# The first layer's gate, s*relu(h)^2 + b, formed whole in the elementwise steps

## The chip, the cores and the metric

One core of a Trainium2 chip runs the whole kernel. The metric is the device time of one execution in microseconds (us); a difference of 2% gets a verdict. The core has a matrix engine (TensorE, PE in the profile; its weight loads are PEld), VectorE (DVE), ScalarE (ACT) and GpSimd (POOL), and an engine that only issues transfers here (SyncE, SP). Each takes its instructions from a queue of its own, in order.

## The reference, cut to what matters

Attention with a memory term gives x; the first layer and the second layer follow. All arrays are float32.

```python
def _moe_ref(x, w_in, w_out, s, b):      # x (2304, 512), w_in (512, 2048), w_out (2048, 512)
    h = x @ w_in
    r = np.maximum(h, 0.0)
    g = s * (r * r) + b                  # s and b: one number each
    return (g @ w_out).astype(np.float32)

def _moe2_ref(x, w_in, w_out):           # the same sizes
    h = x @ w_in
    ...
    g = h * np.tanh(sp)                  # sp = log(1 + exp(h))
    return (g @ w_out).astype(np.float32)
```

Attention has 4 x 8 pairs of batch and head, 576 positions and 64 dimensions of a head.

## The kernel before, in words

**Precision.** TensorE is fed in the 32-bit format `fp32r`. To keep float32 accuracy each operand is split in a high part, rounded to that format, and a low part, the rest; a product takes three matmuls (high x high, high x low, low x high). The splitting is elementwise work: a cast makes the high part, a subtraction the low part.

**Stages.** Attention is done in units, one for a batch and head; batch 0 is done first, in smaller pieces, the other 24 units follow. Meanwhile the weights of the first layer, which arrive as 64-bit words, are converted (`convert`, L602 to L631: load by SyncE into one of the `raw` buffers, two steps on ScalarE, L609 and L614, two on VectorE, L616 and L617, an addition on GpSimd, L619). As soon as the first 256 columns of x are there, the first layer starts between the units of attention. When attention is done, the first layer has TensorE to itself, while the weights of the second layer are converted in the same way and stored to DRAM (L631); there are two `raw` and two `w` buffers, and the load of a conversion stands in SyncE's queue behind the store of an earlier one. Then they are read back, split (L640, L642), and the second layer runs.

**The first layer.** It goes over 9 blocks of 256 tokens (j) and in each over 16 chunks of 128 of the 2048 hidden columns (fc), 144 chunks in all. For a chunk TensorE makes h in a bank of PSUM (`h`, two banks), three parts of four matmuls (L677). `first` then forms the gate in four steps: ScalarE writes relu(h) to `rt` (L705), VectorE multiplies max(h, 0) by it (L706, which also frees the bank), ScalarE casts to `gh` (L708), VectorE subtracts to `gl` (L709). Three chunks later `y_part` multiplies gh and gl by the output weights `woh` and `wol` (12 matmuls, L722) into y. So the gate that TensorE sees is r*r, without s and b. The factor s is put on when y leaves PSUM (`y_out`, L735 on ScalarE and L737 on VectorE, two each for a block). The term b adds b times the column sum of the output weights to each column of y. `column_sums` makes these sums: VectorE adds all 16 slices of woh and wol into `total` (31 additions of 512 columns, L652 and L654), TensorE sums over partitions by a matmul with `ones` (L670), VectorE picks the diagonal and multiplies by b into `bcs` (L666, L668). When the second layer loads y (`load_y`), the cast to `yh` has bcs as its bias (L767) and the subtraction to `yl` adds it too (L770).

**What sets the order.** No engine chooses at run time. Every step is added to a plan with its engine, an estimated duration, a priority, what it waits for and the buffers it needs. `Plan.order` (L168) plays these estimates through before the program is built: a free engine takes the ready step of lowest priority number, and buffers are rings that are waited for. The order in which steps are taken is the order of the instructions in each queue. `column_sums` has priority 700, the loads of y 450, the conversions of the second layer 655.2, the matmuls of the first layer 1000 and more, its elementwise steps -1. The estimates are those of the code (0.264 us for L705, 0.307 for L708), not those of the chip.

Of the kernel before, what the change touches and what calls it, by code (L numbers as in the profile page):

```python
# [9 lines left out]
F32 = mybir.dt.float32  # L10
# [4 lines left out]
AF = mybir.ActivationFunctionType  # L15
ALU = mybir.AluOpType
# [3 lines left out]
P = 128  # L20
# [32 lines left out]
def dve_us(n, fast=False):  # L53
    return 0.068 + (0.00052 if fast else 0.00104) * n
# [200 lines left out]
def attention_then_two_ffn(ctx: ExitStack, tc: tile.TileContext, qk, qz, vm, beta,  # L255
# [3 lines left out]
    nc = tc.nc  # L259
# [34 lines left out]
    ones = const.tile([P, P], F32, name="ones")  # L294
    igate = const.tile([P, 2, H], F32, name="igate")
    sb = const.tile([P, 2], F32, name="sb")
    bcs = const.tile([P, NCC], F32, name="bcs")
# [8 lines left out]
    sums_in = Buf()  # L306
# [10 lines left out]
    nc.scalar.activation(ones, mask[:, :P], AF.Copy, bias=1.0)  # L317
# [327 lines left out]
    def column_sums(prio):  # L645

        total, ps = Buf(R["total"], [P, 512]), Buf(R["o2"], [P, 512])

        def more(r, j, nm):
            x = W[1, nm, r].t[:, j, :].bitcast(F32)  # L650
            if r == j == 0 and nm == "wol":
                nc.vector.tensor_tensor(total.t, W[1, "woh", 0].t[:, 0, :].bitcast(F32), x, op=ALU.add)  # L652
            elif r + j:
                nc.vector.tensor_tensor(total.t, total.t, x, op=ALU.add)  # L654

        for r in range(NR):
            for j in range(FPR):
                def pair(r=r, j=j):
                    more(r, j, "woh")
                    more(r, j, "wol")  # L660

                add(DVE, dve_us(512) * (2 if r + j else 1), prio, pair, [W[1, "woh", r], W[1, "wol", r]] + [total] * (r + j > 0), [total])

        def pick():
            for ec in range(NCC):
                nc.vector.tensor_tensor_reduce(total.t[:, ec * P:(ec + 1) * P], ps.t[:, ec * P:(ec + 1) * P], ident, 1.0, 0.0,  # L666
                                               ALU.mult, ALU.add, bcs[:, ec:ec + 1])
            nc.vector.tensor_scalar(bcs, bcs, sb[:, 1:2], None, op0=ALU.mult)  # L668

        add(PE, 0.87, prio, lambda: nc.tensor.matmul(ps.t, ones, total.t, start=True, stop=True), [total], [ps])  # L670
        add(DVE, 1.0, prio, pick, [ps, total], [sums_in, total])

# [23 lines left out]
    def first(j, fc, prio, ew):  # L696
# [8 lines left out]
        add(ACT, 0.264, ew, lambda: nc.scalar.activation(rt.t, ph.t[:, :N1], AF.Relu), [ph], [rt])  # L705
        add(DVE, 0.335, ew, lambda: nc.vector.scalar_tensor_tensor(rt.t, ph.t[:, :N1], 0.0, rt.t, op0=ALU.max, op1=ALU.mult),  # L706
            [ph, rt], [rt])
        add(ACT, 0.307, ew, lambda: nc.scalar.copy(gh.t, rt.t), [rt], [gh])  # L708
# [214 lines left out]
```

## Time and profile before

| what | us |
|---|---|
| median of three runs (lowest, highest) | 1129.08 (1126.43, 1130.62) |
| the profiled execution: its time | 1132.63 |
| the profiled execution: span from first to last instruction | 1130.5 |
| TensorE busy | 1066.4 (94%) |
| VectorE busy | 686.3 (61%) |
| ScalarE busy | 545.1 (48%) |
| GpSimd busy | 279.7 (25%) |

A share of busy time is a mean over stages that differ: up to about 509 us attention with the first layer between, to about 715 us the first layer alone, then the second. TensorE's matmuls overlap, so that its busy time says little of how near it is to its peak; its waits say more. Three kinds of rows are read below: busy time in a stretch, what ended an engine's idle time ("PE h L677 <- DVE rt L706" reads: the matmul of line 677 waited for the rt that VectorE writes in line 706), and the chain of work that ended last, followed back from the end.

### The profile page before, as it was taken

The numbers are of one execution on the slowest core, as the hardware profiler recorded it, in microseconds if no ns is written. First come the engines' busy times: TensorE is split into PE (matmuls) and PEld (weight loads), VectorE is DVE, ScalarE is ACT, GpSimd is POOL, SyncE is SP. The second block draws the span as 40 slices with busy tenths as digits, with TensorE's granted clock in tenths as the row PEclk, the third lists the DMA queues.
The fourth block names the chain that finished last, engine by engine and source line by source line (L and its number), as shares of the span: only waits on it lengthen the run. The fifth ranks groups of instructions, "written<-read, shape, count | busy, mean of one in ns | idle before, by whom it ended". The sixth has DMA issues, their size and how long they took to land.

```text
span 1130.5 us, 19718 instructions
## 1 busy us (share of the span) xinstructions
PE 1066.4 (94%) x6868; PEld 969.1 (86%) x6868; DVE 686.3 (61%) x2071; ACT 545.1 (48%) x1343; POOL 279.7 (25%) x361
## 2 busy tenths in 40 slices
PE   5879999998999999999899999999999999999998
PEld 3446788997989998998889999999999999999997
DVE  6898999999889888899964334632223232232221
ACT  6576887778778787774553324521112121111111
POOL 5763554455354534442221000000000000000000
PEclk9578999999999999999999999999999999999999
DMA  8463653534334432356563102500101000000000
GB/s 250 131 192 105 187 175 109 152 111 145 102 90 137 137 111 81 112 165 182 177 216 112 39 1 94 179 27 1 56 1 57 1 29 29 1 28 1 28 1 28
DMA packets 54963, 106.80 MB, mean 94 GB/s; under 512 B 6992, under 2 KB 34640, under 8 KB 54864
## 3 DMA queue, kind: packets, MB, share of 16 engines
q1 hardware_dynamic: 54864, 105.54, 30.3%
q8 instruction: 54, 0.88, 0.3%
q14 instruction: 45, 0.37, 0.1%
HBM read 82.97 MB, written 22.54 MB: 93 GB/s over the span
## 4 chain that ended last, share of the span: by engine, by line
PE 59%; DVE 13%; POOL 6%; ACT 6%; issue 5%; DMA 4%; SPq 0%; POOLq 0%; ACTq 0%; DVEq 0%
PE h L677 27%; PE o L795 17%; PE y L722 6%; POOL Pt L486 4%; PE o L722 2%; PE a L541 2%; PE a L513 2%; DVE gl L709 1%; DVE PTl L521 1%; DMA raw<-in_w_in 1%; ACT Pt L469 1%; DVE total L654 1%; DMA raw<-in_w_out 1%; DVE w L617 1%; DVE rt L706 1%
## 5 line engine op out<-in xcount | busy, mean ns | idle before, releaser
L784 ACT ACTIVATE g<-h 128x384 f32<-128x384 f32 x96 | 47.1, 491 | 309.2 <-PE h L677 285.7
L785 DVE CAST gh<-g 128x384 fp32r<-128x384 f32 x96 | 34.6, 361 | 263.6 <-ACT g L784 262.7
L513 PE MATMUL a<-ident,Pt 128*128 128x128 f32 x432 | 76.0, 295 | 31.9 <-POOL Pt L486 26.5
L619 POOL TENSOR_TENSOR w<-w,raw 128x512 int32<-128x512 int32 x54 | 72.9, 1349 | 123.5 <-DVE w L617 68.6
L677 PE MATMUL h<-xh,wih 128*128 128x256 f32 x576 | 95.1, 289 | 8.6 <-DVE rt L706 8.6
L486 POOL TENSOR_SCALAR Pt<-Pt,rs 128x64 f32<-128x64 f32 (+2 forms) x88 | 82.6, 963 | 66.1 <-DVE rs L491 50.4
L677 PE MATMUL h<-xl,wih 128*128 128x256 f32 x576 | 95.2, 287 | 0.1
L677 PE MATMUL h<-xh,wil 128*128 128x256 f32 x576 | 94.8, 287 | 0.0
L513 PEld LDWEIGHTS a<-ident,Pt 128*128 128x128 f32 x432 | 49.8, 146 | 51.8 <-POOL Pt L486 42.2
L469 ACT ACTIVATE Pt<-Pt,mx 128x64 f32<-128x64 f32 (+4 forms) x148 | 81.6, 552 | 23.4 <-DVE mx L460 23.0
L706 DVE SCALAR_TENSOR_TENSOR rt<-h,rt 128x256 f32<-128x256 f32 x144 | 60.4, 419 | 49.6 <-ACT rt L705 48.7
L709 DVE TENSOR_TENSOR gl<-rt,gh 128x256 fp32r<-128x256 f32 x144 | 69.4, 483 | 34.5 <-ACT gh L708 13.5
L677 PEld LDWEIGHTS h<-xh,wih 128*128 128x128 f32 x576 | 79.6, 193 | 11.6 <-DVE rt L706 11.0
L708 ACT CAST gh<-rt 128x256 fp32r<-128x256 f32 x144 | 58.2, 405 | 61.5 <-DVE rt L706 57.0
L472 POOL TENSOR_SCALAR Pt<-ex,nm 128x64 f32<-128x64 f32 x148 | 67.6, 469 | 77.4 <-PE a L513 37.7
L705 ACT ACTIVATE rt<-h 128x256 f32<-128x256 f32 x144 | 54.9, 381 | 59.6 <-PE h L677 56.6
L677 PE MATMUL h<-yh,wih 128*128 128x384 f32 x384 | 82.7, 337 | 0.0
L677 PE MATMUL h<-yl,wih 128*128 128x384 f32 x384 | 82.7, 337 | 0.0
L677 PE MATMUL h<-yh,wil 128*128 128x384 f32 x384 | 82.7, 337 | 0.0
L677 PEld LDWEIGHTS h<-xl,wih 128*128 128x128 f32 x576 | 80.2, 192 | 1.0 <-DVE xl L693 0.4
L677 PEld LDWEIGHTS h<-xh,wil 128*128 128x128 f32 x576 | 79.7, 192 | 0.9 <-issue 0.8
L795 PE MATMUL o<-wol,gh 128*128 128x512 f32 x285 | 80.3, 390 | 0.0
(177 smaller groups left out, 2565.7 us busy)
## 6 DMA issues: line engine op xcount, KB each, us to landing
qk<-in_qk SPq DMA_DIRECT2D x24, 608.0 KB, 3.9
raw<-in_w_out SPq DMA_DIRECT2D x28, 512.0 KB, 3.9
raw<-in_w_in SPq DMA_DIRECT2D x26, 512.0 KB, 4.8
qn<-in_qz SPq DMA_DIRECT2D x29, 192.0 KB, 2.4
vx<-in_vm SPq DMA_DIRECT2D x29, 160.0 KB, 2.4
xr<-x_d SPq DMA_DIRECT2D x36, 128.0 KB, 2.8
y_d<-ys SPq DMA_DIRECT2D x36, 128.0 KB, 1.7
yr<-y_d SPq DMA_DIRECT2D x24, 192.0 KB, 2.7
```

Source lines behind the costliest of these rows:

```text
L469: nc.scalar.activation(Pt[t].t[:, D:w + D], Pt[t].t[:, D:w + D], AF.Exp, bias=mx.t[:, t + i:t + i + 1], scale=-1.0, accum_out=rs.t[:, t:t ...
L472: add(POOL, 0.3, lambda: nc.gpsimd.tensor_scalar(Pt[t].t[:, :D], ex.t[:, t, :], nm.t[:, t:t + 1], 1.0, op0=ALU.mult, op1=ALU.mult), [ex, n ...
L486: (nc.vector if e == DVE else nc.gpsimd).tensor_scalar(x, x, r, None, op0=ALU.mult)
L513: nc.tensor.transpose(ps.t[:, c - c0, :], Pt[t].t[:, c * P:(c + 1) * P], ident)
L619: add(POOL, 1.23, prio, lambda: nc.gpsimd.tensor_tensor(w.t, w.t, words()[:, :, 0], op=ALU.add), [raw, low_words, w], [w])
L677: nc.tensor.matmul(ph, W[layer, nm, r].t[:, cc, o:o + P], x[:, cc], start=(part == 0 and cc == 0), stop=(part == 2 and cc == NCC - 1))
L705: add(ACT, 0.264, ew, lambda: nc.scalar.activation(rt.t, ph.t[:, :N1], AF.Relu), [ph], [rt])
L706: add(DVE, 0.335, ew, lambda: nc.vector.scalar_tensor_tensor(rt.t, ph.t[:, :N1], 0.0, rt.t, op0=ALU.max, op1=ALU.mult), [ph, rt], [rt])
L708: add(ACT, 0.307, ew, lambda: nc.scalar.copy(gh.t, rt.t), [rt], [gh])
L709: add(DVE, dve_us(N1), ew, lambda: nc.vector.tensor_tensor(gl.t, rt.t, gh.t.bitcast(F32), op=ALU.subtract), [rt, gh], [gl])
L722: nc.tensor.matmul(acc[ec // 2].t[:, (ec % 2) * N1:(ec % 2 + 1) * N1], W[1, nm, r].t[:, jj, ec * P:(ec + 1) * P], x.t, start=False, stop=( ...
L795: nc.tensor.matmul(acc[i].t, x.t[:, i * P:(i + 1) * P], W[2, nm, r].t[:, jj, :], start=(fc == 0 and part == 0), stop=(fc == NFC - 1 and pa ...
```

## The change

The gate is made whole: ScalarE writes s*h to `rt` (Copy with a scale read from memory), VectorE multiplies max(h, 0) by it, ScalarE adds b while it casts to `gh` (Identity with a bias read from memory), and VectorE adds b and subtracts gh in one step with three operands. `column_sums`, its tiles and its matmul are gone, y is copied out of PSUM without s, and y is loaded without a bias. Priorities and estimated durations of the steps that stay are as before.

```diff
-    ones = const.tile([P, P], F32, name="ones")
...
-    bcs = const.tile([P, NCC], F32, name="bcs")
...
-    nc.scalar.activation(ones, mask[:, :P], AF.Copy, bias=1.0)
...
-    def column_sums(prio):
-
-        total, ps = Buf(R["total"], [P, 512]), Buf(R["o2"], [P, 512])
...
-                add(DVE, dve_us(512) * (2 if r + j else 1), prio, pair, [W[1, "woh", r], W[1, "wol", r]] + [total] * (r + j > 0), [total])
...
-        add(PE, 0.87, prio, lambda: nc.tensor.matmul(ps.t, ones, total.t, start=True, stop=True), [total], [ps])
-        add(DVE, 1.0, prio, pick, [ps, total], [sums_in, total])
...
-        add(ACT, 0.264, ew, lambda: nc.scalar.activation(rt.t, ph.t[:, :N1], AF.Relu), [ph], [rt])
+        add(ACT, 0.264, ew, lambda: nc.scalar.activation(rt.t, ph.t[:, :N1], AF.Copy, scale=sb[:, 0:1]), [ph], [rt])
         add(DVE, 0.335, ew, lambda: nc.vector.scalar_tensor_tensor(rt.t, ph.t[:, :N1], 0.0, rt.t, op0=ALU.max, op1=ALU.mult),
             [ph, rt], [rt])
-        add(ACT, 0.307, ew, lambda: nc.scalar.copy(gh.t, rt.t), [rt], [gh])
-        add(DVE, dve_us(N1), ew, lambda: nc.vector.tensor_tensor(gl.t, rt.t, gh.t.bitcast(F32), op=ALU.subtract), [rt, gh], [gl])
+        add(ACT, 0.307, ew, lambda: nc.scalar.activation(gh.t, rt.t, AF.Identity, bias=sb[:, 1:2]), [rt], [gh])
+        add(DVE, dve_us(N1), ew, lambda: nc.vector.scalar_tensor_tensor(gl.t, rt.t, sb[:, 1:2], gh.t.bitcast(F32),
+                                                                        op0=ALU.add, op1=ALU.subtract), [rt, gh], [gl])
...
-                nc.scalar.activation(ys.t, src, AF.Copy, scale=sb[:, 0:1])
+                nc.scalar.copy(ys.t, src)
             else:
-                nc.vector.tensor_scalar(ys.t, src, sb[:, 0:1], None, op0=ALU.mult)
+                nc.vector.tensor_copy(ys.t, src)
...
-            add(ACT, 0.41, prio, lambda c=c, yr=yr: nc.scalar.activation(yh.t[:, c], yr.t, AF.Identity, bias=bcs[:, c:c + 1]),
-                [yr, sums_in], [yh, half])
+            add(ACT, 0.41, prio, lambda c=c, yr=yr: nc.scalar.copy(yh.t[:, c], yr.t), [yr], [yh, half])
...
-                lambda c=c, yr=yr: nc.vector.scalar_tensor_tensor(yl.t[:, c], yr.t, bcs[:, c:c + 1], yh.t[:, c].bitcast(F32),
-                                                                  op0=ALU.add, op1=ALU.subtract), [yr, half], [yl])
+                lambda c=c, yr=yr: nc.vector.tensor_tensor(yl.t[:, c], yr.t, yh.t[:, c].bitcast(F32), op=ALU.subtract),
+                [yr, half], [yl])
...
-    rings(m2a, opened, yr=4, yh=2, yl=2, g=1, gh2=1, gl2=1, total=1)
+    rings(m2a, opened, yr=4, yh=2, yl=2, g=1, gh2=1, gl2=1)
...
-    column_sums(700.0)
```

Up to the first addition of the column sums, right after attention, every engine has the same instructions in the same order before and after, but for `ones` and for the forms that changed; GpSimd's order is the same throughout. From there to the end of the first layer the plan comes out differently.

VectorE before, from the last chunk ahead of the first column sum (rt and gl are the gate's steps, w a conversion of the second layer's weights, total the column sums):

```order
L706 SCALAR_TENSOR_TENSOR rt_7471<-h_7421,rt_7471 128x256
L652 TENSOR_TENSOR total_7486<-woh_0_425,wol_0_433 128x512
L709 TENSOR_TENSOR gl_7498<-rt_7471,gh_7490 128x256
L654 TENSOR_TENSOR total_7486<-total_7486,woh_0_425 128x512
L654 TENSOR_TENSOR total_7486<-total_7486,wol_0_433 128x512
L616 TENSOR_SCALAR w_1_7511<-w_1_7511 128x512
```

The same place after the change (yl is the low part of y for the second layer; line numbers are those of the changed kernel):

```order
L674 SCALAR_TENSOR_TENSOR rt_7468<-h_7418,rt_7468 128x256
L677 SCALAR_TENSOR_TENSOR gl_7493<-rt_7468,sb,gh_7485 128x256
L612 TENSOR_SCALAR w_1_7504<-w_1_7504 128x512
L613 SCALAR_TENSOR_TENSOR w_1_7504<-raw_7436,w_1_7504 128x512
L674 SCALAR_TENSOR_TENSOR rt_7519<-h_7470,rt_7519 128x256
L738 TENSOR_TENSOR yl_7535<-yr_7466,yh_7522 128x384
L738 TENSOR_TENSOR yl_7535<-yr_7476,yh_7522 128x384
L677 SCALAR_TENSOR_TENSOR gl_7551<-rt_7519,sb,gh_7537 128x256
L738 TENSOR_TENSOR yl_7535<-yr_7483,yh_7522 128x384
L738 TENSOR_TENSOR yl_7535<-yr_7491,yh_7522 128x384
L674 SCALAR_TENSOR_TENSOR rt_7561<-h_7514,rt_7561 128x256
```

The additions into total are gone, and the loads of y, which had to wait for bcs, stand where they were.

ScalarE before, some chunks later (L609 and L614, writing w and raw, are the two steps of a conversion; ys are evacuations of y):

```order
L705 ACTIVATE rt_7806<-h_7769 128x256
L609 ACTIVATE w_1_7817<-raw_7765 128x512
L614 ACTIVATE raw_7765<-raw_7765 128x512
L708 CAST gh_7838<-rt_7806 128x256
L735 ACTIVATE ys_7852<-y_0_6969,sb 128x256
L705 ACTIVATE rt_7860<-h_7808 128x256
L609 ACTIVATE w_0_7884<-raw_7828 128x512
L708 CAST gh_7890<-rt_7860 128x256
L705 ACTIVATE rt_7895<-h_7854 128x256
L614 ACTIVATE raw_7828<-raw_7828 128x512
L735 ACTIVATE ys_7909<-y_0_6969,sb 128x256
```

ScalarE after, at the corresponding place (L605 and L610 are these two steps):

```order
L673 ACTIVATE rt_7651<-h_7608,sb 128x256
L676 ACTIVATE gh_7664<-rt_7651,sb 128x256
L605 ACTIVATE w_1_7670<-raw_7585 128x512
L610 ACTIVATE raw_7585<-raw_7585 128x512
L673 ACTIVATE rt_7689<-h_7654,sb 128x256
L605 ACTIVATE w_0_7699<-raw_7644 128x512
L610 ACTIVATE raw_7644<-raw_7644 128x512
L676 ACTIVATE gh_7717<-rt_7689,sb 128x256
```

In the piece of before two conversions stand over three chunks (three `rt`), in that of after over two. Counted from the first changed place to the last conversion, 16 conversions stand over 27 chunks before and over 23 after.

## Rows read from the trace of the kernel before

**Rows 1.** Busy time by stage; columns: stretch in us, then engines, clock, DMA
```profile
100.00:509.00 409.00, 384.61 (x2913) 358.04 (x2913) 366.58 (x1307) 317.11 (x832) 193.75 (x256) 0.99 0.43 130
509.00:590.00 81.00, 72.29 (x567) 68.86 (x566) 69.67 (x133) 41.61 (x94) 20.55 (x15) 1.00 0.61 187
590.00:697.00 107.00, 107.00 (x888) 106.75 (x888) 42.74 (x97) 37.53 (x92) 4.11 (x4) 1.00 0.19 64
...
740.00:1131.00 391.00, 386.78 (x1956) 352.24 (x1954) 98.85 (x210) 60.39 (x121) 0.00 (x0) 1.00 0.06 19
```

**Rows 2.** What PE waited for, 100 to 509: us in total, times, longest
```profile
PE a L513 <- POOL Pt L486: 17.6, 35, 2.5
```

**Rows 3.** The same, 509 to 597
```profile
PE h L677 <- DVE rt L706: 7.0, 10, 1.8
PE o L670 <- DVE total L654: 1.6, 1, 1.6
```

**Rows 4.** Groups by line, 100 to 509: busy us, mean ns; idle before, releaser
```profile
L709 DVE TENSOR_TENSOR gl<-rt,gh 128x256 fp32r<-128x256 f32 x73 | 36.5, 502 | 8.5 <-ACT gh L708 3.8 <-PE y L722 2.2 <-ACT Pt L484 1.2
...
L708 ACT CAST gh<-rt 128x256 fp32r<-128x256 f32 x73 | 29.4, 404 | 8.2 <-PE y L722 4.1 <-DVE rt L706 4.0
L705 ACT ACTIVATE rt<-h 128x256 f32<-128x256 f32 x73 | 27.9, 383 | 12.8 <-PE h L677 9.9 <-DVE gl L709 1.4 <-PE a L455 0.8
...
L735 ACT ACTIVATE ys<-y,sb 128x256 f32<-128x256 f32 x8 | 3.8, 474 | 0.2
```

**Rows 5.** The same groups view, 715 to 1131
```profile
L786 DVE TENSOR_TENSOR gl<-g,gh 128x384 fp32r<-128x384 f32 x96 | 53.6, 558 | 9.8 <-PE o L795 1.0 <-DVE gh L785 0.5
...
L770 DVE SCALAR_TENSOR_TENSOR yl<-yr,bcs,yh 128x384 fp32r<-128x384 f32 x16 | 9.5, 614 | 10.4 <-PE h L677 10.4
L767 ACT ACTIVATE yh<-yr,bcs 128x384 fp32r<-128x384 f32 x16 | 8.6, 606 | 8.9 <-PE h L677 8.9
```

**Rows 6.** Timeline of ACT, back-to-back instructions: start us, length us
```profile
587.71 1.00 ACT L692 CAST xh<-xr 128x256 fp32r<-128x256 f32 x3
...
788.33 2.14 ACT L767 ACTIVATE yh<-yr,bcs 128x384 fp32r<-128x384 f32 x4 [2.22 <-PE h L677]
```

**Rows 7.** Chain that ended last, two units of attention: start us, length us
```profile
434.11 0.28 ACT rt L705
...
444.29 0.42 DVE gl L709
...
447.59 0.28 ACT rt L705
```

**Rows 8.** Groups view, 509 to 590, one of the two column-sum lines
```profile
L654 DVE TENSOR_TENSOR total<-total,woh 128x512 f32<-128x512 f32 x15 | 13.6, 907 | 0.0
```

**Rows 9.** Timeline of PE: matmul of the sums, and a later wait
```profile
553.43 1.12 PE L670 MATMUL o<-total,ones 128*128 128x512 f32 x2 [1.63 <-DVE total L654]
...
589.02 0.74 PE L677 MATMUL h<-xh,wih 128*128 128x256 f32 x4 [1.75 <-DVE rt L706]
```

**Rows 10.** Timeline of POOL: conversions after the sums (start us, length us, idle before)
```profile
561.34 1.31 POOL L619 TENSOR_TENSOR w<-w,raw 128x512 int32<-128x512 int32 x1 [4.55 <-ACT rt L705]
...
588.85 1.31 POOL L619 TENSOR_TENSOR w<-w,raw 128x512 int32<-128x512 int32 x1 [1.23 <-ACT xh L692]
...
597.57 1.31 POOL L619 TENSOR_TENSOR w<-w,raw 128x512 int32<-128x512 int32 x1 [1.74 <-ACT raw L614]
...
603.75 1.32 POOL L619 TENSOR_TENSOR w<-w,raw 128x512 int32<-128x512 int32 x1 [4.88 <-DVE w L617]
```

**Rows 11.** Timeline of ACT: a conversion waits for its load, a relu behind it
```profile
575.59 0.67 ACT L609 ACTIVATE w<-raw 128x512 f32<-128x512 f32 x1 [2.48 <-DMA raw<-in_w_in]
...
576.74 0.37 ACT L705 ACTIVATE rt<-h 128x256 f32<-128x256 f32 x1
```

**Rows 12.** Timeline of PE at the change of layer
```profile
715.36 0.74 PE L677 MATMUL h<-xh,wih 128*128 128x256 f32 x4 [0.20 <-DVE rt L706]
```

**Rows 13.** Busy time, a short stretch of attention
```profile
410.00:415.00 5.00, 3.35 (x21) 2.92 (x20) 3.41 (x9) 2.67 (x8) 4.77 (x6) 0.83 0.37 115
```

More of the change, by code (lines that the diff above doesn't have):

```diff
@@ L305, in attention_then_two_ffn @@
     w2_in = {k: Buf() for k in W2D}
-    sums_in = Buf()
     nc.sync.dma_start(igate[:, 1], beta.partition_broadcast(P))
@@ L643, in split_second @@
             [raw, half], [lo])
-    def column_sums(prio):
-        total, ps = Buf(R["total"], [P, 512]), Buf(R["o2"], [P, 512])
[L649 to L660, printed above, removed]
-                add(DVE, dve_us(512) * (2 if r + j else 1), prio, pair, [W[1, "woh", r], W[1, "wol", r]] + [total] * (r + j > 0), [total])
[L664 to L668, printed above, removed]
-        add(PE, 0.87, prio, lambda: nc.tensor.matmul(ps.t, ones, total.t, start=True, stop=True), [total], [ps])
-        add(DVE, 1.0, prio, pick, [ps, total], [sums_in, total])
     def mm_in(ph, layer, xh, xl, fc, part):
```

## Prediction

> **What bounds the kernel now.** I read the stages first. Between 100 and 509 us attention runs, with first-layer matmuls filling TensorE between its own: TensorE is busy 384.6 of 409 us, VectorE 366.6, ScalarE 317.1 [rows 1]. From 509 to 590 TensorE falls to 72.3 of 81 us; from 590 on it is busy without a gap, in the first layer and in the second [rows 1]. So an elementwise instruction can only cost or give time before 590 us, and briefly at the change of layer. Then I read who ends TensorE's waits. In attention it is mostly GpSimd's scaling of the scores, 17.6 us in 35 waits [rows 2], the end of a loop that goes through ScalarE and VectorE once in each unit. From 509 to 597 it is VectorE alone: `rt` late by 7.0 us in ten waits, and 1.6 us for the matmul of the column sums [rows 3]. Last the chain of work: it passes one `rt` of ScalarE and one `gl` of VectorE in each unit of attention, 13.48 us apart from one `rt` to the next [rows 7].
>
> **The changed instructions, one by one.** The new `rt` on ScalarE is Copy with a scale read from `sb`. That very form, same size and also from PSUM, stands in the trace as the scaling of y: 474 ns, against 383 for the relu [rows 4]. So +91 ns. The new `gh` adds a bias read from `sb`. The form stands at 384 columns in the second layer's input, 606 ns [rows 5], and three plain casts of 256 columns take 1.00 us together, so start 0.30 us apart, where four of 384 with a bias take 2.14 us, so start 0.51 us apart [rows 6]. Had a plain cast of 384 columns the spacing of 256 times one and a half, 0.45 us, the operand would cost 60 ns; had it no more than 0.30, 210 ns. I take the +91 ns that was measured at equal size for the scale, which lies between, in length and in spacing alike. The new `gl` gets a third operand: 614 ns against 558 for the plain subtraction of 384 columns [rows 5], +56 ns. Together 182 ns of ScalarE and 56 ns of VectorE for each of the 144 chunks. The scaled evacuations of y become plain copies and give back the same 91 ns, but only 18 times on ScalarE. In the second layer the y tiles lose their bias operand, under a busy TensorE [rows 1], which hides it; their cost is nothing there. One activation of 128 columns at the start (`ones`) goes; it can give no more than its own length, below the relu's 383 ns, and I take nothing.
>
> **Attention, 100 to 509 us.** The order of every engine is the same up to the first column sum, so only lengths change here: 73 chunks [rows 4], 73 x 182 ns = 13.3 us more for ScalarE and 73 x 56 ns = 4.1 us more for VectorE. On the chain there is one `rt` and one `gl` in each 13.48 us [rows 7], 91 + 56 = 147 ns, and 409 / 13.48 = 30.3 such turns: **+4.5 us**. Bounds: 0 if the loop has slack that this one chain does not show, since TensorE's own work covers 94% of the stretch; 13.3 if all that ScalarE gains in work ends up on the path. I take the chain's count, the row nearest to the end that is asked for. Behind a longer `rt` on ScalarE stand the exponentials and the casts of the transposes, and GpSimd waits for their sums.
>
> **Column sums, 509 to 597 us.** Two groups of 15 additions, 13.6 us busy in one of them and nearly the same in the other [rows 8], leave VectorE, with the first sum, the four reductions and the scaling. What they cost TensorE is what it waited: 7.0 + 1.6 us, and the matmul itself, 1.1 us [rows 3, 9]: **-9.7 us** if nothing else is late. But something is next. In the same stretch the second layer's weights are converted, and ScalarE and VectorE hold `rt` behind conversion steps in one queue: the one at 575.59 stood 2.48 us for its load, with an `rt` behind it at 576.74 [rows 11], and TensorE still waited 1.75 us for an `rt` at 589.02, long after the sums were done [rows 9]. The planner now sees a VectorE without sums and packs the conversions closer: 16 conversions stand over 23 chunks of the first layer, where 27 chunks stood before. A chunk is 24 matmuls, and 888 of them take 107 us [rows 1], so 2.89 us; 23 chunks are 66.5 us, or 4.15 us for a conversion. What a conversion takes when VectorE is free is in the rows after the sums: from 561.34 to 603.75 nine intervals of GpSimd's addition, 4.71 us each; the quickest pair in it, 588.85 to 597.57, 4.36 us [rows 10]. So 16 conversions want 75.4 us, or 69.8 at the quickest pace, where TensorE has 66.5 us of work: 8.9 or 3.3 us of new waits. I take the middle, **+6.1 us**. Bounds: 0 if loads land sooner with GpSimd and the store released sooner, 8.9 at the mean pace. Late next is thus the load of the weights, through the two `raw` buffers, with SyncE's queue behind it: a load stands there behind the store of the conversion before.
>
> **The change of layer and the rest.** Around 715 us casts of 1024 columns stand in the queues of both engines, and TensorE waited 0.20 us for one `rt` [rows 12]. Some eight chunks pass here with 0.24 us more each; most of it is slack of the two `h` banks. +0.5 us, from 0 to 2. From there TensorE is full [rows 1].
>
> **Sum.** 4.5 - 9.7 + 6.1 + 0.5 = +1.4 us against the profiled execution, which took 1132.6 us (span 1130.5 and 2.1 around it): 1134.0. That execution stood 3.5 us above the median of the runs, 1129.1; carried over, the forecast is **1130.5 us**, no change that a measurement of this kernel can tell, which begins at about 0.5%, 5.6 us.
>
> **Where a page bears on it.** The spacing in [rows 6] says that an operand read from memory costs ScalarE even when instructions follow each other without a gap. The Trainium skill, page "ScalarE: Activation LUTs", section "What ACT_TABLE_LOAD costs", gives about 93 ns for each such operand and also says that back-to-back activations overlap by about 93 ns; read so that the one hides the other, ScalarE's queue would not grow at all. By that rule the attention term would be VectorE's 30.3 x 56 ns = 1.7 us; the rows speak against it, since the spacing grows with the operand.
>
> **Rivals.** *Faster.* The conversions keep up with the closer plan: with sums gone and buffers free sooner, each takes 4.15 us or less, and attention absorbs half of its term: 2.2 - 9.7 + 0.5 = -7.0, 1122.1 us. For it: of VectorE's 69.7 busy us in that stretch the sums were some 27 [rows 1, 8]. Against: 4.36 is the quickest pair seen. Chance 0.17. *Hidden operands.* ScalarE fetches the operand while the instruction before it still runs, so that its queue does not grow, and of attention's term only VectorE's 30.3 x 56 ns = 1.7 us is left, at the change of layer nothing: 1.7 - 9.7 + 6.1 = -1.9, 1127.2 us. Against: the spacing in [rows 6]. Chance 0.08. *Slower.* Attention is bound by ScalarE's in-order queue, with paths beside the chain just as long, so that nearly the whole 13.3 us is paid: 13.3 - 9.7 + 6.1 + 0.5 = +10.2, 1139.3 us. The point is the sum's: it decides from 8.7 us of attention on, some 65% of ScalarE's added work. For it: ScalarE is busy 78% in a fixed order, and VectorE 90% [rows 1]. A longer gap also lowers the clock: in one such stretch TensorE was busy 3.35 of 5 us and the granted clock was 0.83 [rows 13], a stretch partly at 1.2 GHz, some 0.9 us lost each time. The Trainium skill, "TensorE: Matmul & The Clock Gate", section "What's actually happening", says that a gate halves the clock of an array that is not kept busy; by it, as the row shows, lost time would bring some more. Against: TensorE has work of its own for 94% of the stretch. Chance 0.28. The forecast itself keeps 0.47.
>
> **How the numbers follow.** The likeliest is 1130.5. Its own bounds, with conversions between 3.3 and 8.9 us and attention between 2 and 8, are 1125 to 1137. To hold 8 in 10 the range reaches into both outer rivals: 1122.5 to 1139. Faster by over 0.5% is the first rival, 0.17, less a little of it that falls short, 0.15. Slower by over 0.5% is the slow rival and the forecast's own upper edge, 0.32. Within 0.5%: 0.53.
>
> **What would show it.** In the profile after: `rt` near 474 ns, `gh` near 495 and `gl` near 540 in attention; the end of attention some 4 to 5 us later than 509; TensorE's waits for `rt` between there and the last conversion about 6 us, beginning only when a few conversions have run, with ScalarE's conversion steps waiting for loads; and from there on the same lengths as before. I am wrong in the attention term if its end moves by under 1 or over 9 us, in the conversion term if TensorE's waits there are under 2 us or over 10, and in the plan if waits appear after the change of layer.

## Result: 1140.1 us, slower by 0.8%

| | before | after |
|---|---|---|
| median of the runs, us | 1129.45 | 1140.12 |
| lowest to highest, us | 1126.43 to 1130.62 | 1137.99 to 1140.95 |
| profiled execution / its span, us | 1132.6 / 1130.5 | 1140.95 / 1139.2 |

The ratio is 1.0081, with a 95% interval of 1.0055 to 1.0108: slower, clear of the noise, but by less than the 2% that gets a verdict. The forecast was 1130.5 and its range ended at 1139.0; the time lies 1.1 us above it. In the lines of after, `rt` is L673 (ScalarE) and L674 (VectorE), `gh` L676, `gl` L677, the matmuls of h are L645 and those of the second layer's o L763.

Busy time by stage, after, in the columns of [rows 1] (stretch, then PE, PEld, DVE, ACT and POOL with their counts, granted clock, DMA share, GB/s):

```profile
100.00:509.00 409.00, 383.55 (x2901) 355.35 (x2900) 371.81 (x1307) 328.09 (x830) 192.92 (x256) 0.99 0.43 129
509.00:590.00 81.00, 74.95 (x585) 73.35 (x585) 51.06 (x100) 49.31 (x102) 22.34 (x18) 0.96 0.68 210
590.00:697.00 107.00, 107.00 (x889) 106.74 (x888) 40.91 (x92) 42.33 (x89) 1.51 (x2) 1.00 0.16 50
740.00:1131.00 391.00, 391.00 (x1938) 351.19 (x1937) 96.41 (x209) 57.68 (x120) 0.00 (x0) 1.00 0.05 18
```

Beside [rows 1], ScalarE has 328.1 us in attention where it had 317.1, and VectorE 51.1 of 81 us in the stretch of the column sums where it had 69.7. The last row is the one to look at: TensorE is busy for all of 391 us in the second layer, and yet it gets through 1938 matmuls there, against 1956 in [rows 1], where its work even ended 4 us before the stretch did.

The gate instructions in attention, after, as in [rows 4]:

```profile
L677 DVE SCALAR_TENSOR_TENSOR gl<-rt,sb,gh 128x256 fp32r<-128x256 f32 x73 | 39.7, 544 | 8.0 <-ACT gh L676 4.2 <-PE y L691 3.0 <-issue 0.2
L676 ACT ACTIVATE gh<-rt,sb 128x256 fp32r<-128x256 f32 x72 | 36.5, 508 | 6.3 <-DVE rt L674 2.7 <-PE y L691 1.7 <-PE a L452 1.1
L673 ACT ACTIVATE rt<-h,sb 128x256 f32<-128x256 f32 x73 | 34.5, 472 | 10.9 <-PE h L645 8.2 <-DVE gl L677 1.3 <-PE a L451 0.7
```

TensorE's waits from 509 to 760 us, after, in the columns of [rows 3], which end at 597 us (total us, times, longest):

```profile
PE h L645 <- DVE rt L674: 5.3, 4, 3.5
PE h L645 <- DVE xl L661: 1.7, 2, 1.1
```

To see where 8.7 us of span came from, I split each trace at four events that both kernels have: the first matmul of y, the end of the last matmul with V (attention), the first output matmul of the second layer, and the last one.

| stage, us | before | after | difference | forecast |
|---|---|---|---|---|
| up to the first matmul of y | 106.8 | 107.5 | +0.7 | 0 |
| attention | 398.9 | 399.9 | +1.0 | +4.5 |
| from there to the second layer's first output matmul | 229.0 | 227.3 | -1.7 | -3.1 |
| second layer, first to last output matmul | 391.4 | 400.1 | **+8.7** | 0 |

All of the loss is in the second layer, whose matmuls the diff does not touch. Two timelines of TensorE from the middle of that layer (start us, length us, then the instruction and its count), first before, then after:

```profile
851.69 0.84 PE L795 MATMUL o<-wol,gh 128*128 128x512 f32 x3
852.37 0.86 PE L677 MATMUL h<-yh,wih 128*128 128x384 f32 x4
853.07 0.84 PE L795 MATMUL o<-woh,gl 128*128 128x512 f32 x3
```

```profile
851.26 0.87 PE L763 MATMUL o<-woh,gl 128*128 128x512 f32 x3
851.97 0.87 PE L645 MATMUL h<-yh,wil 128*128 128x384 f32 x4
852.68 0.87 PE L763 MATMUL o<-woh,gh 128*128 128x512 f32 x3
```

Four h matmuls and three o matmuls took 1.38 us before (851.69 to 853.07) and take 1.42 after (851.26 to 852.68). The groups of the whole layer (740 to 1120 us; count, then busy us, mean ns, idle us) show the same, with no idle time in either:

```profile
L677 PE MATMUL h<-yh,wih 128*128 128x384 f32 x368 | 79.3, 337 | 0.0
...
L795 PE MATMUL o<-woh,gh 128*128 128x512 f32 x275 | 77.5, 390 | 0.0
```

```profile
L645 PE MATMUL h<-yh,wih 128*128 128x384 f32 x360 | 78.2, 338 | 0.0
...
L763 PE MATMUL o<-woh,gh 128*128 128x512 f32 x268 | 77.6, 397 | 0.0
```

The granted clock is 1.00 in both, so this is no fall to 1.2 GHz. Every matmul is simply a little further from the next. In ns from start to start, the mean over 760 to 1110 us is 197.4 before and 201.8 after; the layer has some 1980 such steps (391.4 us / 197.4 ns), and 1980 x 4.4 ns = 8.7 us. Some three quarters of it lie in the output matmuls: from the start of one to the next start it is 227.5 ns before and 235.6 after, at the h matmuls 174.8 and 176.7. What had changed for these matmuls? Their instructions and their order are the same. But two constants ahead of the weights are gone (the ones matrix, 512 bytes in each partition, and the four bias columns, 32 with their padding), and so the weights and the gate's buffers behind them lie 544 bytes lower: the weights begin at byte 18912 instead of 19456. The experiments test that.

### The profile page after: what moved, and what is told of

Its sections match the earlier page's. It is cut to its first block, busy times and chain, and to the rows that moved or that the text cites. A ratio compares the mean times of both kernels' runs of the same rounds, so it can differ in the third digit from the quotient of the medians.

```text
span 1139.2 us, 19632 instructions
## 1 busy us (share of the span) xinstructions
PE 1075.0 (94%) x6866; PEld 972.2 (85%) x6866; DVE 669.4 (59%) x2031; ACT 567.2 (50%) x1342; POOL 277.2 (24%) x361
## 4 chain that ended last, share of the span: by engine, by line
PE 59%; DVE 12%; ACT 6%; DMA 6%; POOL 6%; issue 5%; SPq 1%; POOLq 0%; ACTq 0%; DVEq 0%
PE h L645 26%; PE o L763 18%; PE y L691 6%; POOL Pt L482 4%; PE o L691 3%; PE a L537 2%; DMA raw<-in_w_in 2%; DVE PTl L517 2%; PE a L509 2%; DMA raw<-in_w_out 2%; ACT Pt L465 1%; DVE gl L677 1%; DVE Pt L456 1%; ACT PTh L514 1%; POOL w L615 1%
## 5 line engine op out<-in xcount | busy, mean ns | idle before, releaser
L645 PE MATMUL h<-xh,wih 128*128 128x256 f32 x576 | 95.4, 290 | 6.9 <-DVE rt L674 6.7
L673 ACT ACTIVATE rt<-h,sb 128x256 f32<-128x256 f32 x144 | 67.9, 471 | 62.8 <-PE h L645 60.0
L677 DVE SCALAR_TENSOR_TENSOR gl<-rt,sb,gh 128x256 fp32r<-128x256 f32 x144 | 76.8, 534 | 37.0 <-ACT gh L676 33.1
L645 PE MATMUL h<-xl,wih 128*128 128x256 f32 x576 | 95.7, 288 | 1.7 <-DVE xl L661 1.7
L674 DVE SCALAR_TENSOR_TENSOR rt<-h,rt 128x256 f32<-128x256 f32 x144 | 60.5, 420 | 59.2 <-ACT rt L673 58.9
L645 PE MATMUL h<-xh,wil 128*128 128x256 f32 x576 | 94.6, 287 | 0.0
L676 ACT ACTIVATE gh<-rt,sb 128x256 fp32r<-128x256 f32 x144 | 73.1, 508 | 40.7 <-DVE rt L674 37.1
L645 PEld LDWEIGHTS h<-xh,wih 128*128 128x128 f32 x576 | 80.4, 194 | 8.6 <-DVE rt L674 8.2
L645 PE MATMUL h<-yh,wil 128*128 128x384 f32 x384 | 83.4, 338 | 0.0
L645 PE MATMUL h<-yl,wih 128*128 128x384 f32 x384 | 83.4, 338 | 0.0
L645 PE MATMUL h<-yh,wih 128*128 128x384 f32 x384 | 83.4, 338 | 0.0
L645 PEld LDWEIGHTS h<-xl,wih 128*128 128x128 f32 x576 | 80.6, 193 | 2.7 <-DVE xl L661 2.1
L763 PE MATMUL o<-woh,gh 128*128 128x512 f32 x285 | 82.4, 397 | 0.0
L763 PE MATMUL o<-wol,gh 128*128 128x512 f32 x285 | 82.4, 397 | 0.0
```

What stands on the lines that cost most here:

```text
L645: nc.tensor.matmul(ph, W[layer, nm, r].t[:, cc, o:o + P], x[:, cc], start=(part == 0 and cc == 0), stop=(part == 2 and cc == NCC - 1))
L676: add(ACT, 0.307, ew, lambda: nc.scalar.activation(gh.t, rt.t, AF.Identity, bias=sb[:, 1:2]), [rt], [gh])
L677: add(DVE, dve_us(N1), ew, lambda: nc.vector.scalar_tensor_tensor(gl.t, rt.t, sb[:, 1:2], gh.t.bitcast(F32), op0=ALU.add, op1=ALU.subtract ...
L763: nc.tensor.matmul(acc[i].t, x.t[:, i * P:(i + 1) * P], W[2, nm, r].t[:, jj, :], start=(fc == 0 and part == 0), stop=(fc == NFC - 1 and pa ...
```

## Experiments

**The tiles' place.** A pad tile moves what lies behind it. The first four move the left side of memory: the weights, and behind them the first layer's buffers, later the second layer's gate buffers. The diff of the first (in the third it has 16 columns, and the second makes the same edit in the kernel before):

```
     sb = const.tile([P, 2], F32, name="sb")
+    pad = const.tile([P, 8], F32, name="pad")
```

> The changed kernel with one unused tile of 32 bytes per partition behind sb, so that everything allocated behind it, the weights first, starts 32 bytes later: at byte 18944, a multiple of 64, as in the kernel before (19456), instead of 18912. Order and instructions are those of the changed kernel. Address theory (the second layer's matmuls are slower because the weights they stream start 32 bytes past a multiple of 64): the second layer returns to 1.38 us for seven matmuls from 1.41, its span shrinks by 8.6 us, and the time falls to about 1131 us, ratio to before near 1.001. Rival (the second layer is slower because of what runs beside it, the plain loads of y): nothing changes, 1140 us. Rival (the absolute position of the tiles, 544 bytes lower, matters): at 512 lower most of the loss stays, above 1136 us.

Measured: 1129.05 us, 0.9978 of the kernel before (0.9954 to 1.0002). The second layer takes 392.5 us. Both rivals miss: what runs beside the layer is the same as in the changed kernel, and the tiles are still 512 bytes lower than before.

> The kernel before with the same unused tile of 32 bytes, so that its weights start at byte 19488, 32 past a multiple of 64. Nothing else differs. Address theory: the second layer grows by 8 to 9 us, to 1.41 us for seven matmuls, and the time rises to about 1138 us; the stages up to the end of the first layer stay within 1.5 us. Rival (what runs beside the second layer): no change, 1129 us. Rival (absolute position): 32 bytes are too little to matter, 1129 us.

Measured: 1131.45 us, 1.0011 (0.9988 to 1.0035); second layer 393.9 us. The kernel before loses 2.5 us there, not 9.

> The changed kernel with an unused tile of 64 bytes instead of 32: everything behind it moves twice as far, but again 32 past a multiple of 64. Address theory (only the place within 64 bytes counts): as slow as the changed kernel, 1138 to 1141 us, seven matmuls of the second layer in 1.41 us. Rival (absolute position, any move away from the changed kernel's places helps): faster, below 1136 us.

Measured: 1131.33 us, 1.0016 (0.9983 to 1.0048); second layer 393.3 us. These weights lie 32 past a multiple of 64, as those of the changed kernel do, and the pace is nearly the quick one. A plain rule of alignment to 64 bytes falls with it.

In the fourth a second pad, behind the weights, moves the buffers another 32 bytes. They lie 32 past a multiple of 64 then, as in the changed kernel, but not at their place there: 480 bytes below that of the kernel before, where the changed kernel has them 544 below. So against the first experiment the buffers alone move, whatever the run's name says:

```
+    pad = const.tile([P, 8], F32, name="pad")
...
+    mpad = ctx.enter_context(tc.tile_pool(name="mpad", bufs=1)).tile([P, 8], F32, name="mpad")
     first_layer = ExitStack()
```

> The changed kernel with the weights at a multiple of 64 and the tiles behind them (x and gate tiles of the first layer, later three of the four gh and gl of the second) put back to 32 past one by a second unused tile of 32 bytes. It tells which operand of the second layer's matmuls counts: the weights, which are streamed in the output matmul (512 columns), or gh and gl, which are loaded as the stationary side there. If the streamed weights: 0.68 us for three output matmuls and about 1131 us in all. If the stationary gh and gl: 0.71 us and about 1139 us. Each a part: in between.

Measured: 1129.24 us, 0.9991 (0.996 to 1.0023). The second layer takes 396.4 us, half-way; but the first layer got quicker. TensorE in the first layer alone and in the second (stretch, busy us and count, granted clock, DMA share, GB/s), in the first experiment and then with the buffers 32 bytes further:

```profile
600.00:700.00 100.00, 100.00 (x832) 1.00 0.10 31
740.00:1120.00 380.00, 379.72 (x1924) 1.00 0.05 18
```

```profile
600.00:700.00 100.00, 100.00 (x856) 1.00 0.13 41
740.00:1120.00 380.00, 380.00 (x1903) 1.00 0.05 17
```

In the same 100 us the first layer passes 856 matmuls instead of 832, and the second loses 21 of 1924. Both are at clock 1.00 and full, but for 0.28 us.

Two kernels move the right side of memory by 32 bytes (the second layer's input y, a few buffers and, in attention, its tiles), by a pad ahead of the pool `stage`: the kernel before, and the changed kernel on top of the first pad.

> The kernel before with an unused tile of 32 bytes at the other end of the memory, so that the tiles allocated from there start 32 bytes lower: yh and yl, which the second layer's first matmul streams (384 columns), at a multiple of 64 instead of 32 past one; in attention the tiles move too, some to a multiple of 64, some away from one. Address theory, if it holds for every streamed operand: the four h matmuls of the second layer get shorter than 0.70 us and the time falls by up to 8 us. Rival (only what the output matmul streams counts, since the h matmuls wait for their weight loads): the second layer stays at 0.70 us, the time within 2 us of before.

Measured: 1133.73 us, 1.0016 (0.9994 to 1.0038); second layer 393.3 us.

> The changed kernel with both unused tiles, so that weights and the y tiles start at multiples of 64. If the streamed y tiles count: the time of the changed kernel with the weights moved (about 1131 us) less what the other kernel with the right end moved gained, so down to 1123 us. If they do not: about 1131 us.

Measured: 1132.41 us, 1.0003 (0.998 to 1.0026); second layer 395.6 us, where the same left side gave 392.5.

So far the slow pace of 400 us had been seen in one trace alone. It could still have been the chip or the loading. The next three ran on one chip, beside the same runs of the kernel before: the changed kernel as it is; the kernel before with only its two constants laid behind the weights, so that the weights begin at 18912; and the changed kernel with the second pad alone, which has its weights at 18912 too, and its buffers 512 bytes lower than before has them.

> The changed kernel once more, unchanged, on the chip and beside the runs of the kernels below. In its first trace seven matmuls of the second layer take 1.41 us, and 400.1 us pass from the first to the last output matmul of that layer; in the eight other kernels run so far they take 391.4 to 396.4 us. Theory 'place': the pace follows from where the tiles lie in on-chip memory, so it repeats: 399.5 to 400.5 us again, median 8 to 11 us above the kernel before (ratio 1.007 to 1.010). Rival 'chance': the pace belongs to one chip or one loading, and is lost here: 391 to 396 us, median 1128 to 1133 us.

Measured: 1140.59 us, 1.0088 (1.0057 to 1.0118); second layer 400.9 us. It repeats, on another loading, and the rival of chance falls.

```
     wpool = ctx.enter_context(tc.tile_pool(name="w", bufs=1))
+    const2 = ctx.enter_context(tc.tile_pool(name="const2", bufs=1))
...
-    ones = const.tile([P, P], F32, name="ones")
+    ones = const2.tile([P, P], F32, name="ones")
...
-    bcs = const.tile([P, NCC], F32, name="bcs")
+    bcs = const2.tile([P, NCC], F32, name="bcs")
```

> The kernel before with its ones matrix and its four bias columns laid behind the weights instead of ahead of them: the weights then lie at byte 18912, exactly where the changed kernel has them, and everything else stays where the kernel before has it; no work is added or taken away. Theory 'place', if the weights' own place decides: 396 to 400 us for the second layer (391.4 before), median 4 to 9 us above the kernel before. If it needs the gate's buffers moved as well: 391 to 394 us, within 3 us of before. Rival 'change': the slower pace comes from the changed instructions: 391.4 us and no change of the median.

Measured: 1134.58 us, 1.0041 (1.0016 to 1.0067); second layer 397.7 us. No work was added or taken away, and the kernel before loses 6.3 us in the layer where the changed one lost 8.7. Its first layer alone gets quicker, but the stage between attention and the second layer stays at 229.0 us: from 509 to 760 us TensorE waits 10.2 us for `rt` there, in the kernel before 7.2.

> The changed kernel with 32 bytes ahead of the first layer's buffers alone: the weights stay at byte 18912, the second layer's gate buffers move by 32 to a multiple of 64. Its pair is the run in which only the weights were moved (396.4 us for the second layer). Theory 'place', weights decide: 396 to 400 us, median 4 to 9 us above the kernel before; gate buffers decide: 391 to 394 us, median 1127 to 1131 us. Should it equal the run of the kernel before with its weights at this same byte, the change itself has no part in the pace.

Measured: 1132.77 us, 1.0025 (1.0001 to 1.005); second layer 398.1 us. The same two stretches for the kernel before, the changed kernel again, the kernel before with its weights moved, and the changed kernel with its buffers moved:

```profile
600.00:700.00 100.00, 100.00 (x832) 1.00 0.14 48
740.00:1120.00 380.00, 380.00 (x1927) 1.00 0.05 18
```

```profile
600.00:700.00 100.00, 100.00 (x832) 1.00 0.11 35
740.00:1120.00 380.00, 380.00 (x1884) 1.00 0.05 17
```

```profile
600.00:700.00 100.00, 100.00 (x852) 1.00 0.16 51
740.00:1120.00 380.00, 380.00 (x1896) 1.00 0.05 18
```

```profile
600.00:700.00 100.00, 100.00 (x855) 1.00 0.12 40
740.00:1120.00 380.00, 380.00 (x1896) 1.00 0.05 17
```

The last two have different instructions in the first layer and the same 1896 matmuls in 380 us of the second. Their weights lie at the same byte, their buffers 512 bytes apart, and they run alike, so the pace goes with the place and not with the change. Nor does the gate's form have a part in it: in the table three kernels with all tiles at the same places and three different gates (the first experiment, e6 and f4) take 391.4 to 392.5 us. Putting the weights at 18912 costs 6 us of the 8.7, and moving the buffers too costs the rest. All rows of this kind together (bytes against the kernel before; us; the stages as above). The second layer has four pairs of gate buffers; that column stands for three of them, and the fourth lies on the right side. In all changed kernels two of the four load buffers of y on the right side also lie 2048 bytes higher, since `total` is gone.

| kernel | weights | gate buffers | right side | attention | middle | second layer |
|---|---|---|---|---|---|---|
| before | 0 | 0 | 0 | 398.9 | 229.0 | 391.4 |
| e2_before_w_moved_32 | +32 | +32 | 0 | 398.8 | 230.4 | 393.9 |
| e7_before_right_moved_32 | 0 | 0 | -32 | 399.9 | 229.6 | 393.3 |
| f2_before_w_only | -544 | 0 | 0 | 400.9 | 229.0 | 397.7 |
| after | -544 | -544 | 0 | 399.9 | 227.3 | 400.1 |
| f1_after_again | -544 | -544 | 0 | 403.1 | 225.5 | 400.9 |
| e1_after_w_moved_32 | -512 | -512 | 0 | 402.1 | 225.6 | 392.5 |
| e3_after_moved_64 | -480 | -480 | 0 | 402.4 | 225.0 | 393.3 |
| e8_after_both_moved_32 | -512 | -512 | -32 | 402.8 | 225.9 | 395.6 |
| e4_after_w_only | -512 | -480 | 0 | 400.4 | 221.3 | 396.4 |
| f3_after_gate_buffers_only | -544 | -512 | 0 | 400.4 | 221.4 | 398.1 |
| e5_before_gate_only | 0 | 0 | 0 | 405.1 | 230.7 | 391.9 |
| e6_sums_gone_plain_gate | -512 | -512 | 0 | 399.5 | 225.5 | 392.0 |
| f4_only_b_in_gate | -512 | -512 | 0 | 399.7 | 224.6 | 391.4 |

That the place sets the pace is shown. Which rule of addresses does it is not: no single distance in the table sorts the last column, and a move of 32 or 64 bytes can give 1 us or 8. Two regularities stand in the rows. Kernels whose places differ by 512 bytes alone run alike (before and e5 against e1, e6 and f4: 391.4 to 392.5 us; e2 and e3: 393.9 and 393.3; f2 and f3: 397.7 and 398.1), but the last such pair, e7 and e8, does not (393.3 and 395.6). And the first layer alone goes by one distance: with the buffers 32 or 544 bytes further from the weights than in the kernel before (e4, f3, f2) it passes 852 to 856 matmuls in 100 us, and in the kernels that keep the distance 832, but for e2, which has a wait of 0.6 us in that stretch.

**The gate by itself.** The kernel before, with its three gate instructions in their new form and nothing else changed:

```
-        add(ACT, 0.264, ew, lambda: nc.scalar.activation(rt.t, ph.t[:, :N1], AF.Relu), [ph], [rt])
+        add(ACT, 0.264, ew, lambda: nc.scalar.activation(rt.t, ph.t[:, :N1], AF.Copy, scale=sb[:, 0:1]), [ph], [rt])
...
-        add(ACT, 0.307, ew, lambda: nc.scalar.copy(gh.t, rt.t), [rt], [gh])
+        add(ACT, 0.307, ew, lambda: nc.scalar.activation(gh.t, rt.t, AF.Identity, bias=sb[:, 1:2]), [rt], [gh])
```

(and `gl` as in the change).

> The kernel before with only the three gate instructions of the change (Copy with scale, Identity with bias, the subtraction with three operands); column sums, scaling and bias of y stay, and so do order and addresses. Its output carries s twice and b in the gate as well as in the bias, so it is a different function of the same work. It measures the price of the operands alone. Forecast's term: attention ends 4.5 us later than before (chain's count), and the stretch with the column sums, where VectorE and ScalarE are behind, gets some of 27 x 0.24 us, so the time is 5 to 8 us above before. Rival (the other work of TensorE absorbs the operands, as the end of attention in the changed kernel suggests, 1.7 us late): under 2 us above before in attention, under 4 in all. Rival (ScalarE's queue is the bound): 13 us or more.

Measured: 1137.51 us, 1.0050 (1.0032 to 1.0068), so some 5.7 us on 1131.4, the median of the kernel before beside it. Its gate in attention, and its waits from 509 to 760 us:

```profile
L709 DVE SCALAR_TENSOR_TENSOR gl<-rt,sb,gh 128x256 fp32r<-128x256 f32 x72 | 39.5, 549 | 6.6 <-ACT gh L708 4.2 <-PE y L723 1.7 <-PE h L677 0.2
L708 ACT ACTIVATE gh<-rt,sb 128x256 fp32r<-128x256 f32 x72 | 36.4, 507 | 6.1 <-DVE rt L706 3.5 <-PE y L723 1.9 <-PE a L456 0.6
L705 ACT ACTIVATE rt<-h,sb 128x256 f32<-128x256 f32 x72 | 34.0, 472 | 11.1 <-PE h L677 8.1 <-DVE gl L709 1.7 <-PE a L455 0.7
```

```profile
PE h L677 <- DVE rt L706: 8.5, 12, 1.5
PE o L670 <- DVE total L654: 1.9, 1, 1.9
```

The three instructions have the lengths that they have in the changed kernel. The waits are those of [rows 3], 8.5 and 1.9 us, where the kernel before has 7.2 and 1.6 in this longer stretch, and attention takes 405.1 us, 6.2 more than in the trace of before. No other kernel pays as much there.

**The sums by themselves.** The changed kernel on the first pad with the plain gate of before, so that s and b are left out altogether:

> The changed kernel with the plain gate of the kernel before (relu, cast, two-operand subtraction), so without s and b anywhere, and with the weights at a multiple of 64 again. It measures what the removal of the column sums and of the bias of y gives by itself, in the changed order. Forecast's term: the waits of TensorE from 509 to 597 fall from 8.6 to about 6 us and the matmul of 1.1 us goes, 3 to 4 us below before. Rival (VectorE's backlog was all there was): 9 to 10 us below before. Rival (the closer packed conversions cost as much as the sums): within 2 us of before.

Measured: 1124.07 us, 0.9918 (0.9889 to 0.9948), from four runs. Its waits from 509 to 760 us:

```profile
PE h L646 <- DVE rt L675: 4.7, 5, 2.0
PE h L646 <- DVE xl L662: 1.7, 2, 1.1
```

In its trace the middle stage is 3.5 us shorter than in the kernel before and attention 0.6 us longer. Of the 8.0 us by which its span is shorter, 5.7 lie ahead of that: this execution begins its first matmul of y at 101.1 us instead of 106.8. That start moves between executions of one kernel (107.5 and 103.2 in the two traces of the changed one). Whether it was as early in the other three runs no trace shows, so I take the trace's stage as the price, and the ratio's 9.3 us as an upper one.

**Half of the gate.** The last kernel, on the first pad, takes s out of the gate again: y is scaled as before, the gate adds b/s, and ScalarE's first instruction is a plain relu.

```
+    nc.vector.reciprocal(pad[:, 0:1], sb[:, 0:1])
+    nc.vector.tensor_tensor(sb[:, 1:2], sb[:, 1:2], pad[:, 0:1], op=ALU.mult)
...
-        add(ACT, 0.264, ew, lambda: nc.scalar.activation(rt.t, ph.t[:, :N1], AF.Copy, scale=sb[:, 0:1]), [ph], [rt])
+        add(ACT, 0.264, ew, lambda: nc.scalar.activation(rt.t, ph.t[:, :N1], AF.Relu), [ph], [rt])
...
-                nc.scalar.copy(ys.t, src)
+                nc.scalar.activation(ys.t, src, AF.Copy, scale=sb[:, 0:1])
```

> The changed kernel moved by 32 bytes, but with s taken out of the gate again: the gate is relu(h)^2 + b/s (one division at the start), and y is scaled by s as before. ScalarE's first gate instruction is then a plain relu of 383 ns instead of 471, its other two keep the added operand. Computes the same result for s other than zero. By the steps of the prediction attention loses its larger term (91 ns in each of 30.3 turns, 2.8 us), and the 16 scalings of y lie beside other work: median 2 to 4 us below the changed kernel moved by 32, 1125 to 1127 us, ratio 0.994 to 0.997. Rival 'ScalarE is covered': its added time costs nothing in attention, ratio 0.998 as that kernel. Rival 'vector': the cost of the gate, 5.7 us in the run with the gate alone, is VectorE's gl; then also 0.998.

Measured: 1130.52 us, 1.0009 (0.9984 to 1.0034). ScalarE's two gate instructions in attention:

```profile
L679 ACT ACTIVATE gh<-rt,sb 128x256 fp32r<-128x256 f32 x73 | 37.0, 509 | 6.7 <-DVE rt L677 2.9 <-PE y L694 1.8 <-PE a L455 1.2
...
L676 ACT ACTIVATE rt<-h 128x256 f32<-128x256 f32 x73 | 27.9, 383 | 11.1 <-PE h L648 8.3 <-DVE gl L680 1.4 <-PE a L454 0.8
```

The relu is back at its old length, and in the one trace attention is 2.4 us shorter than in the first experiment. The timed runs do not show it: the ratio is not below that kernel's 0.9978, and the intervals overlap. What this half of the gate costs stays open. No kernel that computes the whole result was measurably faster than the kernel before.

## Why the prediction was right in its parts and wrong in its sum

**The prices of the instructions were near.** `rt` takes 472 ns (474 forecast) and `gh` 508 (495): the bias on `gh` costs 104 ns, 13 more than the scale that I took for it. `gl` takes 544, so its third operand costs 42 ns and not 56. The 540 that the prediction names for it does not follow from its own sum, which is 502 + 56 = 558. Nor is the operand hidden behind the instruction ahead of it, as one rival had it. Four plain casts of 384 columns on ScalarE in the changed kernel:

```profile
789.28 1.76 ACT L736 CAST yh<-yr 128x384 fp32r<-128x384 f32 x4 [2.29 <-PE h L645]
```

They start 0.42 us apart, and 0.51 us with the bias [rows 6].

**Attention: the sign was right, the size high.** Forecast +4.5 us. The two traces of the changed kernel give +1.0 and +4.2. Over the four kernels with the plain gate in the order of before (before, two moved ones and the one with the constants moved) attention takes 398.8 to 400.9 us, 399.6 in the mean; over the seven with the full changed gate 399.9 to 403.1, 401.6 in the mean: +2.0 us, though the two groups overlap. The gate by itself gave 405.1, +5.5. So the chain's count of one `rt` and one `gl` per turn was the right order of size, and the bound of 13.3 us, on which the slow rival rested, was not reached by any kernel.

**Column sums and conversions: the size was right, the path in part.** The forecast was -9.7 + 6.1 + 0.5 = -3.1 us for this stage; the change gave -1.7 and in its repeat -3.5, and the three kernels that only moved it, with the same pace in the first layer, -3.1 to -4.0. TensorE waited 5.3 us for `rt` and 1.7 for `xl`, the low part of x, where the sum had 6.1 for the conversions and 0.5 for the change of layer. Not all of it stands where the sum put it. TensorE's waits of over 0.15 us in the changed kernel (start, length, instruction, idle before and its releaser):

```profile
527.15 0.74 PE L645 MATMUL h<-xh,wih 128*128 128x256 f32 x4 [0.77 <-DVE rt L674]
...
529.93 0.38 PE L645 MATMUL h<-xl,wih 128*128 128x256 f32 x1 [0.60 <-DVE xl L661]
...
531.39 1.06 PE L645 MATMUL h<-xl,wih 128*128 128x256 f32 x3 [1.07 <-DVE xl L661]
...
571.59 1.23 PE L645 MATMUL h<-xh,wih 128*128 128x256 f32 x4 [3.47 <-DVE rt L674]
...
714.59 0.74 PE L645 MATMUL h<-xh,wih 128*128 128x256 f32 x4 [0.46 <-DVE rt L674]
...
721.20 0.74 PE L645 MATMUL h<-xh,wih 128*128 128x256 f32 x4 [0.60 <-DVE rt L674]
```

The first three, 2.4 us, are not in the sum. They come from VectorE's queue: `rt` stands there behind a load of y, which no longer waits for bcs, and `xl` behind a conversion:

```profile
526.20 0.56 DVE L738 TENSOR_TENSOR yl<-yr,yh 128x384 fp32r<-128x384 f32 x1 [0.90 <-ACT yh L736]
526.68 0.42 DVE L674 SCALAR_TENSOR_TENSOR rt<-h,rt 128x256 f32<-128x256 f32 x1
...
528.85 0.69 DVE L613 SCALAR_TENSOR_TENSOR w<-raw,w 128x512 int32<-128x512 int32 x1
529.46 0.42 DVE L661 TENSOR_TENSOR xl<-xr,xh 128x256 fp32r<-128x256 f32 x1
```

The fourth, 3.47 us, is the wait that the sum had, and the last two, 1.1 us, are its change of layer. ScalarE just ahead of the fourth, at conversion steps that wait for their load:

```profile
565.43 0.67 ACT L605 ACTIVATE w<-raw 128x512 f32<-128x512 f32 x1 [2.47 <-DMA raw<-in_w_in]
...
569.36 0.66 ACT L605 ACTIVATE w<-raw 128x512 f32<-128x512 f32 x1 [2.29 <-DMA raw<-in_w_in]
```

GpSimd's addition of the last conversion starts at 594.5 us, 9.3 us before the one in [rows 10], and the transfer of the weights is the largest of what is late next, as the prediction said. It left out one cost: after the wait of 3.47 us the clock falls. Three stretches of the changed kernel (five engines, then granted clock, DMA share, GB/s):

```profile
410.00:415.00 5.00, 3.94 (x33) 3.72 (x33) 4.77 (x16) 4.31 (x12) 2.35 (x3) 1.00 0.32 85
573.00:578.00 5.00, 5.00 (x27) 5.00 (x26) 2.53 (x7) 2.83 (x6) 1.29 (x1) 0.53 0.52 158
578.00:583.00 5.00, 5.00 (x44) 5.00 (x43) 2.62 (x6) 2.14 (x5) 1.31 (x1) 1.00 0.71 226
```

At 573 to 578 us the granted clock is 0.53, a stretch almost wholly at 1.2 GHz, after TensorE had idled. It passes 27 matmuls there, and 44 in the next 5 us at 1.00: by this count an estimate of 1.9 us lost. In the repeat that wait was 2.65 us, the clock was 0.66 from 570 to 575 us, and the stage was 1.8 us shorter. In attention it is the other way round: at 410 to 415, where [rows 13] has 0.83, the changed kernel has 1.00. The repeat has 1.00 there too, with TensorE busy for 3.28 of the 5 us where [rows 13] has 3.35, so a gap of that size does not lower the clock each time. All of it lies inside the stages' times above.

**The second layer: wrong, and the whole loss.** The step that failed is the sentence "From there TensorE is full". It is full, in both kernels, and I took that for the same length. A full TensorE runs at a pace of its own, and this moved by 2.2%, 8.7 us, because the tiles moved by 544 bytes. None of the rivals had it. The slow rival gave 1139.3 us, close to the result by luck, since its mechanism did not happen: its 13.3 us of attention were 1 to 4. With the pace nearly restored, by 32 or by 64 bytes of padding, the same change gives 0.9978 and 1.0016, and both intervals hold 1: no change that can be told, as the forecast had it. Its parts, measured apart, are +5.7 us for the gate and between -3.5 and -9.3 for the sums; together they leave room for the forecast's +1.4 as well as for the -2.5 of the first experiment.

## What to carry to other kernels

A change that adds or drops a constant tile also moves every tile behind it; where TensorE is full, compare the count of matmuls in an equal stretch of both traces before explaining a difference by the instructions, and try the change again with a pad of 32 and of 64 bytes. Price an operand by a row of the same form and size, and its effect by how often that instruction stands on the chain, not by the engine's sum of work. When one wait goes, ask which queue's pace comes next: here the load of the weights, and with it VectorE's queue and the clock, took back more than half.

## What the runs showed of the hardware

- At a granted clock of 1.00, and with TensorE busy without a gap, the steps between matmuls depend on where the weights, the buffers and the tiles of the right side lie: 197.4 to 201.9 ns in the mean in the second layer (391.4 to 400.9 us), and in the first layer alone 117.2 to 120.6 ns. The best place for one layer is not the best for the other: the buffers alone moved by 32 bytes gave 856 matmuls in 100 us of the first layer instead of 832, and lost 4 us in the second (396.4 against 392.5).
- The Trainium skill, "SBUF — State Buffer", section "SBUF: two separate sides", says that TensorE's own port never waits on anyone, and "TensorE: Matmul & The Clock Gate", section "Step-by-step: what each phase is for", that loading the next weights takes no read bandwidth of that memory from the running matmul. Neither sentence leads one to expect what the runs show: with work, order and clock alike, the place alone cost the kernel before 6.3 us. Whether weight loads and moving data meet in the memory after all, or something else does it, no run here shows.
- A [128 x 1] operand costs ScalarE 89 ns as a scale (383 to 472) and 104 ns as a bias (404 to 508) at 256 columns. The Trainium skill, "ScalarE: Activation LUTs", section "What ACT_TABLE_LOAD costs", gives about 93 ns, and the trace agrees within 11 ns.
